# Seven dense groups of 384 and 512 tokens, two low halves on another engine, and a shorter check of limits

## The chip, the cores and the metric

The kernel runs on one core of a Trainium2 chip. The metric is the device time of one execution in microseconds (us); lower is better. TensorE is called PE in the profile, with its weight loads listed apart as PEld; DVE is VectorE, ACT is ScalarE, POOL is GpSimd and SP is SyncE, which here issues most of the transfers.

## The reference

Three layers run one after the other on 3072 tokens of width 384 (4 batches of 768 positions, 8 heads of 48).

```
state = alpha[t] * state + k[t] (x) v[t];  y[t] = q[t] . state      # gated linear attention, per head
noisy = x @ w_gate + log1p(exp(x @ w_noise)) * noise                # 8 experts, the best 2 of each token
out[token] += weight * (relu(x @ w1[e]) @ w2[e])                    # w1: 384 x 1024, w2: 1024 x 384
g = max(0.01 * h, h), h = x @ w_in;  result = g @ w_out             # dense layer, 384 -> 2048 -> 384
```

## The kernel before, in words

**Stages.** Attention runs first, in 24 units of 128 positions. Each unit ends in logits; after every four units a routing chain on DVE (lines 229 to 304 and 1216 to 1258) ranks the experts and gives each choice a slot, and POOL scatters the token rows to the slots by indirect DMA (line 1267). Then the eight experts run, each with two groups of tokens of 320 to 512 rows, then the dense layer with eight groups of 384 tokens. The dense layer fetches its rows by indirect DMA from the experts' outputs (`gather2`, line 830).

**Steps of experts and dense layer.** A group is worked in steps of 128 hidden units. In a step `gemm1` (line 751) makes 9 matmuls whose moving width is the number of tokens of the group (three slices of the 384 inputs, each as high x high, high x low, low x high part). `hidden` then splits the result into a high and a low half: for an expert ACT writes the high half (line 769) and DVE the low one (line 779); in the dense layer ACT copies (line 761), and DVE does the leaky rectifier (764), the high half (771) and the low half (782). `gemm2` (line 799, or 795 for a half block) makes three matmuls of width 384 for each block of 128 tokens. It runs two steps behind `gemm1` (`LAG = 2`); `gemm1` writes to one of two banks (`ph`), and a bank is free when the split of two steps before is done. Four banks (`py`) hold the sums of a group's blocks.

**Weights.** Expert weights come in pairs of 256 hidden units, four pairs for an expert. SP fetches a pair's two halves (`w1s`, `w2s`, two buffers each), ACT makes the high part (`split_hi`, line 504) and DVE or POOL the low part (`split_lo`, line 508). For expert 0 all eight low parts are on POOL, for expert 1 on DVE, for the others wherever the planner finds room.

**Order.** A planner (class `Planner`) places every step in order of time, from durations written into the program, dependences, rings of buffers and due times; each engine's instructions are then issued in that order, and an engine waits at the head of its own queue. Steps of phase 1 may be placed while the attention runs.

**Check of limits.** After the first groups a few sums of counts (`flag_sums`, line 625 ff., on PE into the bank `pA`) are compared with the limits for which the fast path is made (`raise_flag`, lines 632 to 652): 18 small operations on DVE in one planner step. If a limit is broken, a general program runs behind.

```
on = "g" if e == 0 else "v" if e < EARLY else "vg"
add("v", 3.0, raise_flag, use=[(v1, R["pA"])], phase=2, due=tm[0] + 60)
groups += [("b", 0, g) for g in range(N // GROUP2)]
```

Of the kernel before, what the change touches and what calls it, by code (L numbers as in the profile page):

```python
# [28 lines left out]
EARLY = 2  # L29
# [7 lines left out]
SURE, CLEARED = 656, 4  # L37
GROUP2 = 384
F64B = 2
# [334 lines left out]
def tile_kernel(  # L374
# [74 lines left out]
    ones_b = consts.tile([128, 128], BF)  # L449
    zeros = consts.tile([128, Dm], FT)  # L450
    acc = consts.tile([128, NCH + 1, E], BF)
# [7 lines left out]
    msk = {}  # L459

    def route_consts():
        nc.gpsimd.iota(desc, pattern=[[1, E]], base=1, channel_multiplier=0, allow_small_or_imprecise_dtypes=True)
        nc.gpsimd.memset(ones_f, float(E))
        for i in range(2):
            nc.gpsimd.tensor_copy(turn_w[:, :, i * D:(i + 1) * D],
                                  identf[:, None, 64 * i:64 * i + D].to_broadcast([128, HP, D]))
        nc.gpsimd.affine_select(out=tri, in_=ones_f, pattern=[[1, 128]], compare_op=OP.is_gt, fill=0.0,
                                base=0, channel_multiplier=-1)
        nc.gpsimd.memset(ones_b, float(E))
        nc.gpsimd.memset(zeros, 0.0)  # L470
# [108 lines left out]
    def clear():  # L579
        ins = nc.sync.dma_start(x_s[1 + E * SURE:1 + E * CAP, :].rearrange("(m p) d -> p m d", p=128),  # L580
                                zeros[:, None, :].to_broadcast([128, E * (CAP - SURE) // 128, Dm]))
        apart(ins, [other for other, tile_no in scattered if tile_no < CLEARED] + [t for t, _ in taken])
        cleared.append(ins)

    def blocks(key):
        return GB[key[1]][key[2]] if key[0] == "a" else blocks_of(GROUP2)

    GMAX = max(max(max(sizes) for sizes in SIZES), GROUP2)
    XT, XP, bank_of = {}, {}, {}
# [42 lines left out]
    def raise_flag():  # L632
        pf = flags["pf"]
        cm = rt.tile([128, 1], FT, name="cmx")
        nc.vector.tensor_reduce(cm, pf[:, 0:E], axis=AX.X, op=OP.max)
        nc.vector.tensor_scalar(cm, cm, float(E * CAP + E), None, op0=OP.is_le)
        vs = rt.tile([128, 1], FT, name="vs")
        nc.vector.tensor_scalar(vs, pf[:, E:E + 1], 0.0, None, op0=OP.is_le)
        nc.vector.tensor_mul(vs, vs, cm)
        nc.vector.tensor_reduce(cm, pf[:, 0:E], axis=AX.X, op=OP.add)  # L640
        nc.vector.tensor_scalar(cm, cm, float(E * 2 * N + E * (E + 1) // 2), None, op0=OP.is_equal)
        nc.vector.tensor_mul(vs, vs, cm)
        nc.vector.tensor_reduce(cm, pf[:, 0:E], axis=AX.X, op=OP.min)
        nc.vector.tensor_scalar(cm, cm, float(E * SURE), None, op0=OP.is_gt)
        nc.vector.tensor_mul(vs, vs, cm)
        nc.vector.tensor_reduce(cm, pf[:, E + 1 + EARLY:], axis=AX.X, op=OP.max)
        nc.vector.tensor_scalar(cm, cm, float(E * SURE + E), None, op0=OP.is_le)
        nc.vector.tensor_mul(vs, vs, cm)
        for e in range(EARLY):
            nc.vector.tensor_scalar(cm, pf[:, E + 1 + e:E + 2 + e], float(E * SIZES[e][0]), None, op0=OP.is_ge)  # L650
            nc.vector.tensor_mul(vs, vs, cm)
        nc.vector.tensor_scalar(flag, vs, -1.0, 1.0, op0=OP.mult, op1=OP.add)


    groups = [("a", e, g) for g in range(2) for e in range(EARLY)]
    groups += [("a", e, g) for e in range(EARLY, E) for g in range(2)]
    groups += [("b", 0, g) for g in range(N // GROUP2)]
    LAG = 2

    def build_experts(t0, R, scat, cleared_at, ready_at, totals, acc_done, begun):  # L660
# [29 lines left out]
        def expert_weights(i, after):  # L690
# [4 lines left out]
            for m, nm in enumerate(("w1s", "w2s")):  # L695
# [57 lines left out]
        def hidden(si, what):  # L753
# [65 lines left out]
        def rows_stored(gi, j):  # L819
            key = groups[gi]  # L820
            o, n = blocks(key)[j]
            r0 = key[2] * GROUP2 + o
            dst = rows_of(y_d, key[1], key[2], j) if key[0] == "a" else out[r0:r0 + n, :]
            nc.sync.dma_start(dst, YG[gi, j][:n, :])

        def gather2(g, j, kk):
            c = g * (GROUP2 // 128) + j
            rows = 1 + (E * G0 if (c + 1) * 128 <= G0 else E * CAP)
# [4 lines left out]
        def combine(g, j, kk):  # L833
            c = g * (GROUP2 // 128) + j
            ya = YG["b", g, j, 0]
            if kk == 0:
                nc.scalar.activation(ya, ya, AF.Copy, scale=wts[:, c, 0:1])
            else:
                nc.vector.scalar_tensor_tensor(ya, YG["b", g, j, 1], wts[:, c, 1:2], ya, op0=OP.mult, op1=OP.add)
                xg_t["b", 0, g, j] = ya  # L840

        out_rows = {0: [], 1: []}
        xdone, S1, S2 = {}, {}, {}
        t = t0

        def group_in(gi):
# [50 lines left out]
        for si, (gi, f, nf) in enumerate(steps):  # L897
# [666 lines left out]
```

## Time and profile before

| | |
|---|---|
| median of 3 runs | 1033.15 us (1027.29 to 1034.31) |
| the profiled execution | 1029.27 us |
| its span, first to last instruction | 1027.6 us |
| what lies around the span | 1.67 us |
| mean granted TensorE clock | 0.997 |
| busy: PE, DVE, ACT, POOL | 98%, 55%, 37%, 27% |

Busy is the share of the span in which an engine had work. Matmuls are pipelined, so the time of a run of matmuls is read from the distance between their starts, not from their durations.

### The profile page before, as it was taken

Reading aid. Unit: us, or ns where it says so; the run is one execution under the profiler, and the core shown is the slowest. Engines: PE = TensorE matmul, PEld = TensorE weight load, DVE = VectorE, ACT = ScalarE, POOL = GpSimd, SP = SyncE. Lnnn points to the kernel's source line nnn. Section 1 sums busy time; section 2 is a strip of 40 time slices with the busy share of each in tenths; the row PEclk is TensorE's granted clock in tenths of the full one; section 3 lists DMA queues with packets and bytes.
Section 4 is the critical chain, followed back from the end, with each engine's and each line's share of the span. In section 5 each row is a group of like instructions: output and inputs, shape, how many; then the busy total and the mean of one; then the engine's idle time right before and its main releaser. Section 6 shows DMA issues by size and latency. Waiting matters only on the chain.

```text
span 1027.6 us, 17907 instructions
## 1 busy us (share of the span) xinstructions
PE 1005.4 (98%) x6714; PEld 968.6 (94%) x6714; DVE 567.5 (55%) x1270; ACT 384.3 (37%) x815; POOL 277.6 (27%) x310
## 2 busy tenths in 40 slices
PE   8999889999999999999999999999999999999997
PEld 7888779999899999999999999999999999999997
DVE  8999946224745545454543456645454545454543
ACT  5667535223534545353533342313131313121211
POOL 4377776001122324242322244302020202000000
PEclk9999999999999999999999999999999999999999
DMA  9979737325533646454667564302020202010000
GB/s 256 248 251 292 253 136 241 117 89 177 188 113 133 211 141 206 143 182 155 190 215 260 180 210 136 95 1 70 1 70 1 70 1 70 1 40 1 24 1 27
DMA packets 79507, 133.37 MB, mean 130 GB/s; under 512 B 8498, under 2 KB 57140, under 8 KB 79412
## 3 DMA queue, kind: packets, MB, share of 16 engines
q1 hardware_dynamic: 73268, 113.26, 34.9%
q0 software_dynamic: 6144, 18.88, 5.5%
q8 instruction: 55, 0.90, 0.4%
q14 instruction: 40, 0.33, 0.1%
HBM read 92.98 MB, written 39.13 MB: 129 GB/s over the span
## 4 chain that ended last, share of the span: by engine, by line
PE 85%; DVE 7%; DMA 3%; POOL 2%; issue 2%; ACT 1%; SPq 0%; POOLq 0%; DVEq 0%; ACTq 0%
PE ph L751 40%; PE py L799 38%; PE py L795 2%; DVE pT L1016 2%; DVE pF L1009 2%; PE pA L600 1%; DMA at<-in_al_l_dram 1%; PE pB L600 1%; POOL x_s L1267 1%; DVE kt L1030 1%; DVE qp L1036 1%; DMA kq<-in_kq_l_dram 1%; DMA x_s<-xg,si 1%; POOL w1lA L508 1%; PE pA L1161 1%
## 5 line engine op out<-in xcount | busy, mean ns | idle before, releaser
L799 PE MATMUL py<-w2hA,hh 128*128 128x384 f32 x768 | 220.0, 340 | 0.0
L799 PE MATMUL py<-w2hB,hh 128*128 128x384 f32 x768 | 218.7, 338 | 0.0
L779 DVE SCALAR_TENSOR_TENSOR hh<-ph,hh 128x64 fp32r<-128x64 f32 (+2 forms) x192 | 79.4, 442 | 182.7 <-ACT hh L769 182.6
L761 ACT ACTIVATE hc<-ph 128x384 f32<-128x384 f32 x128 | 62.9, 491 | 283.2 <-PE ph L751 283.2
L764 DVE SCALAR_TENSOR_TENSOR hc<-hc 128x384 f32<-128x384 f32 x128 | 72.4, 565 | 168.7 <-ACT hc L761 168.4
L769 ACT ACTIVATE hh<-ph 128x384 fp32r<-128x384 f32 (+3 forms) x128 | 66.3, 518 | 233.6 <-PE ph L751 207.5
L799 PEld LDWEIGHTS py<-w2hA,hh 128*128 128x128 f32 x768 | 141.5, 189 | 0.9
L799 PEld LDWEIGHTS py<-w2hB,hh 128*128 128x128 f32 x768 | 140.9, 188 | 0.7
L751 PE MATMUL ph<-xh,w1hA 128*128 128x384 f32 (+3 forms) x384 | 134.7, 351 | 4.6 <-DVE hh L779 2.8
L751 PE MATMUL ph<-xh,w1lA 128*128 128x384 f32 (+3 forms) x384 | 132.9, 346 | 0.3 <-POOL w1lA L508 0.3
L751 PE MATMUL ph<-xh,w1hB 128*128 128x384 f32 (+1 forms) x384 | 132.7, 346 | 0.0
L751 PE MATMUL ph<-xl,w1hB 128*128 128x384 f32 (+1 forms) x384 | 132.5, 345 | 0.1
L751 PE MATMUL ph<-xl,w1hA 128*128 128x384 f32 (+3 forms) x384 | 132.4, 345 | 0.0
L751 PE MATMUL ph<-xh,w1lB 128*128 128x384 f32 (+1 forms) x384 | 132.3, 344 | 0.0
L799 PE MATMUL py<-w2lA,hh 128*128 128x384 f32 x384 | 130.0, 339 | 0.3 <-POOL w2lA L508 0.3
L799 PE MATMUL py<-w2lB,hh 128*128 128x384 f32 x384 | 128.7, 335 | 0.0
L830 POOL DMA_INDIRECT xg<-y_d,gidx x48 | 49.5, 1031 | 248.0 <-PE pA L600 117.7
L751 PEld LDWEIGHTS ph<-xh,w1hA 128*128 128x128 f32 x384 | 72.4, 189 | 7.0 <-DVE hh L779 2.1
L751 PEld LDWEIGHTS ph<-xh,w1lA 128*128 128x128 f32 x384 | 72.4, 189 | 3.0 <-POOL w1lA L508 0.6
L782 DVE TENSOR_TENSOR hh<-hc,hh 128x384 fp32r<-128x384 f32 x128 | 72.5, 566 | 4.4
L751 PEld LDWEIGHTS ph<-xl,w1hA 128*128 128x128 f32 x384 | 72.4, 189 | 1.5
L751 PEld LDWEIGHTS ph<-xh,w1lB 128*128 128x128 f32 x384 | 72.1, 188 | 1.7
(181 smaller groups left out, 1572.4 us busy)
## 6 DMA issues: line engine op xcount, KB each, us to landing
w1s<-in_moe_w_dram SPq DMA_DIRECT2D x32, 384.0 KB
w2s<-in_moe_w_dram SPq DMA_DIRECT2D x32, 384.0 KB
kq<-in_kq_l_dram SPq DMA_DIRECT2D x24, 448.0 KB
xg<-x_s SPq DMA_DIRECT2D x48, 192.0 KB
y_d<-ys SPq DMA_DIRECT2D x48, 192.0 KB
nv<-in_v_l_dram SPq DMA_DIRECT2D x24, 256.0 KB
w1s<-in_moe_w_in_dram SPq DMA_DIRECT2D x24, 256.0 KB
w2s<-in_moe_w_out_dram SPq DMA_DIRECT2D x16, 384.0 KB
```

Of the source, the lines that this page charges most:

```text
L600: pe.last = nc.tensor.transpose(p[:, d, :n], src[:n, d * 128:(d + 1) * 128], identf[:n, :n])
L751: pe.last = nc.tensor.matmul(ps[:, :n], a[:, d, fo:fo + 128], x[:, d, :n], start=i == 0, stop=i == len(seq) - 1)
L761: nc.scalar.activation(hc[:, :n], ps[:, :n], AF.Copy)
L764: nc.vector.scalar_tensor_tensor(hc[:, :n], hc[:, :n], 0.01, hc[:, :n], op0=OP.mult, op1=OP.max)
L769: nc.scalar.activation(hh[:, :n], ps[:, :n], AF.Relu)
L779: nc.vector.scalar_tensor_tensor(dst, ps[:, a:b], 0.0, hh[:, a:b].bitcast(FT), op0=OP.max, op1=OP.subtract)
L782: nc.vector.tensor_sub(hl[:, :n], HT[si, "hc"][:, :n], hh[:, :n].bitcast(FT))
L795: pe.last = nc.tensor.matmul(py, HT[si, "both"][:, o:o + 128], w[:, f % 2, :], start=(f == 0 and i == 0), stop=(f == nf - 1 and i == 1))
L799: pe.last = nc.tensor.matmul(py[:n, :], h[:, o:o + n], w[:, f % 2, :], start=(f == 0 and i == 0), stop=(f == nf - 1 and i == 2))
L830: return nc.gpsimd.indirect_dma_start(out=yg, out_offset=None, in_=y_d[0:rows, :], in_offset=bass.IndirectOffsetOnAxis(ap=gidx[:, c, kk:kk ...
L1009: nc.vector.tensor_tensor_scan(rev(suf_f[:, 0:NW - 1]), rev(d["at"][:, 1:NW]), rev(heads_f[:, 1:NW]), 1.0, OP.mult, OP.add)
L1016: nc.vector.tensor_tensor_scan(wt, d["at"][:, i * half:(i + 1) * half], heads_f[:, i * half:(i + 1) * half], 0.0, OP.mult, OP.add)
```

## The change

Four edits. The dense layer's eight groups of 384 tokens become seven, of 384, 512, 512, 512, 384, 384 and 384 tokens; the planner's durations for the dense splits scale with the width. For the last two pairs of expert 0 the low halves are made on DVE instead of POOL (four operations; the first two pairs stay on POOL). The check of limits becomes two comparisons of all sums with two rows of limits (prepared at the start by POOL), a sum, a comparison, a count and the flag: six operations, each a planner step of its own. The tile of zeros moves to a pool that ends with the attention.

```diff
-GROUP2 = 384
+GROUPS2 = (384, 512, 512, 512, 384, 384, 384)
...
+    roof, base_ = (consts.tile([128, 2 * E + 1 + EARLY], FT, name=nm) for nm in ("roof", "base_"))
...
-        nc.gpsimd.memset(zeros, 0.0)
+        nc.gpsimd.memset(short["zeros"], 0.0)
...
+        nc.gpsimd.memset(roof, BIG)
+        nc.gpsimd.memset(base_, -BIG)
+        nc.gpsimd.memset(roof[:, 0:E], float(E * CAP + E))
...
+        def above():
+            nc.vector.tensor_tensor(bad[:, 0:n], pf, roof, op=OP.is_gt)
+
+        def below():
+            nc.vector.tensor_tensor(bad[:, n:2 * n], pf, base_, op=OP.is_lt)
+
+        def summed():
+            nc.vector.tensor_reduce(total[:, 0:1], pf[:, 0:E], axis=AX.X, op=OP.add)
+
+        def missing():
+            nc.vector.tensor_scalar(bad[:, 2 * n:], total[:, 0:1], float(E * 2 * N + E * (E + 1) // 2), None, op0=OP.not_equal)
+
+        def counted():
+            nc.vector.tensor_reduce(total[:, 1:2], bad, axis=AX.X, op=OP.add)
+
+        def raised():
+            nc.vector.tensor_scalar(flag, total[:, 1:2], 0.0, None, op0=OP.is_gt)
...
-    groups += [("b", 0, g) for g in range(N // GROUP2)]
+    groups += [("b", 0, g) for g in range(len(GROUPS2))]
...
-                on = "g" if e == 0 else "v" if e < EARLY else "vg"
+                on = "g" if e == 0 and PAIRS[i][2] < 2 else "v" if e < EARLY else "vg"
...
-                hc = HT[si, "hc"] = mw.tile([128, GROUP2], FT, name="hc", bufs=2)
+                hc = HT[si, "hc"] = mw.tile([128, max(GROUPS2)], FT, name="hc", bufs=2)
...
-                hc = add("a", 0.5, lambda si=si: hidden(si, "hc"), use=[(g1, R["ph"])], takes=[R["hc"]], phase=2)
-                lk = add("v", 0.6, lambda si=si: hidden(si, "leak"), use=[(hc, R["hc"])], phase=2)
+                hc = add("a", 0.5 * k, lambda si=si: hidden(si, "hc"), use=[(g1, R["ph"])], takes=[R["hc"]], phase=2)
+                lk = add("v", 0.6 * k, lambda si=si: hidden(si, "leak"), use=[(hc, R["hc"])], phase=2)
...
-                add("v", 3.0, raise_flag, use=[(v1, R["pA"])], phase=2, due=tm[0] + 60)
+                fo = add("v", 0.0, lambda: parts.extend(raise_flag()), [v1], phase=2, due=tm[0] + 60)
+                for k in range(6):
+                    fo = add("v", 0.17, lambda k=k: parts[k](), [fo], use=[(v1, R["pA"])] if k < 3 else [], phase=2,
+                             due=tm[0] + 60 + k)
...
+        zeros = short["zeros"] = ac.tile([128, Dm], FT, name="zeros")
```

## Rows read from the trace of the kernel before

**Rows 1.** The page: busy time by engine, and the chain that ended last.

```profile
PE 1005.4 (98%) x6714; PEld 968.6 (94%) x6714; DVE 567.5 (55%) x1270; ACT 384.3 (37%) x815; POOL 277.6 (27%) x310
PE 85%; DVE 7%; DMA 3%; POOL 2%; issue 2%; ACT 1%; SPq 0%; POOLq 0%; DVEq 0%; ACTq 0%
```

**Rows 2.** Windows: stretch, length, busy us (instructions) by engine, clock, DMA, GB/s.

```profile
140.00:150.00 10.00, 7.30 (x37) 6.75 (x35) 8.53 (x20) 4.72 (x10) 8.18 (x7) 0.83 0.65 213
200.00:225.00 25.00, 25.00 (x132) 22.33 (x131) 5.75 (x10) 5.57 (x11) 0.00 (x0) 1.00 0.35 114
```

**Rows 3.** Timeline of DVE, 264 to 272 us: start, length, operation [idle before].

```profile
264.64 0.17 DVE L635 TENSOR_REDUCE cmx<-pA 128x1 f32<-128x8 f32 x1 [0.66 <-PE pA L630]
...
265.68 1.87 DVE L642 TENSOR_TENSOR vs<-vs,cmx 128x1 f32<-128x1 f32 x1
...
269.95 0.16 DVE L648 TENSOR_TENSOR vs<-vs,cmx 128x1 f32<-128x1 f32 x1
...
270.99 1.01 DVE L779 SCALAR_TENSOR_TENSOR hh<-ph,hh 128x384 fp32r<-128x384 f32 x2
```

**Rows 4.** Timeline of PE, 269 to 272 us.

```profile
269.45 0.34 PE L799 MATMUL py<-w2hB,hh 128*128 128x384 f32 x1
271.59 0.44 PE L751 MATMUL ph<-xh,w1hA 128*128 128x384 f32 x1 [1.80 <-DVE hh L779]
```

**Rows 5.** Timeline of PE, 144 to 162 us: the first matmul behind each wait.

```profile
144.66 0.38 PE L751 MATMUL ph<-xh,w1hA 128*128 128x320 f32 x1 [1.84 <-ACT hh L769]
...
150.10 0.39 PE L751 MATMUL ph<-xh,w1hA 128*128 128x320 f32 x1 [0.95 <-DVE hh L779]
...
159.58 0.41 PE L751 MATMUL ph<-xh,w1lA 128*128 128x320 f32 x1 [0.31 <-POOL w1lA L508]
...
161.36 0.44 PE L799 MATMUL py<-w2lA,hh 128*128 128x384 f32 x1 [0.32 <-POOL w2lA L508]
```

**Rows 6.** Timeline of POOL, 142 to 164 us: low halves of expert 0.

```profile
142.15 1.84 POOL L508 TENSOR_TENSOR w2lA<-w2s,w2hA 128x768 fp32r<-128x768 f32 x1
...
146.43 1.85 POOL L508 TENSOR_TENSOR w1lA<-w1s,w1hA 128x768 fp32r<-128x768 f32 x1
...
157.68 1.85 POOL L508 TENSOR_TENSOR w1lA<-w1s,w1hA 128x768 fp32r<-128x768 f32 x1
159.47 3.62 POOL L508 TENSOR_TENSOR w2lA<-w2s,w2hA 128x768 fp32r<-128x768 f32 x2
```

**Rows 7.** Timeline of DVE, 141 to 157 us.

```profile
141.47 2.58 DVE L240 SCALAR_TENSOR_TENSOR g_um<-g_u,g_ex 128x32 f32<-128x32 f32 x1
...
145.77 2.58 DVE L302 SCALAR_TENSOR_TENSOR g_rest<-g_oh,g_z 128x32 f32<-128x32 f32 x1
...
149.41 1.01 DVE L779 SCALAR_TENSOR_TENSOR hh<-ph,hh 128x64 fp32r<-128x64 f32 x4
152.16 0.56 DVE L779 SCALAR_TENSOR_TENSOR hh<-ph,hh 128x64 fp32r<-128x64 f32 x2 [1.75 <-ACT hh L769]
...
155.87 0.95 DVE L508 TENSOR_TENSOR w1lB<-w1s,w1hB 128x768 fp32r<-128x768 f32 x1
```

**Rows 8.** Timeline of ACT, 143 to 159 us: two high halves of expert 0.

```profile
143.12 0.84 ACT L504 ACTIVATE w1hA<-w1s 128x768 fp32r<-128x768 f32 x1 [0.94 <-DMA w1s<-in_moe_w_dram]
...
157.65 0.84 ACT L504 ACTIVATE w2hA<-w2s 128x768 fp32r<-128x768 f32 x1
```

**Rows 9.** Chain of waits: start, length, nine matmuls of one gemm1.

```profile
199.65 2.08 PE ph L751 x9
...
671.86 1.56 PE ph L751 x9
...
704.36 1.59 PE ph L751 x9
```

**Rows 10.** Groups by line: busy us, mean ns, idle before and its releaser.

```profile
L764 DVE SCALAR_TENSOR_TENSOR hc<-hc 128x384 f32<-128x384 f32 x128 | 72.4, 565 | 168.7 <-ACT hc L761 168.4
```

**Rows 11.** Timeline of POOL at the start.

```profile
9.60 1.24 POOL L1080 TENSOR_SCALAR_AFFINE_SELECT am<-ar 128x512 f32<-128x512 f32 x2 [5.43 <-ACT ar L1075]
```

More of the change, by code (lines that the diff above doesn't have):

```diff
@@ L449, in tile_kernel @@
     ones_b = consts.tile([128, 128], BF)
-    zeros = consts.tile([128, Dm], FT)
     acc = consts.tile([128, NCH + 1, E], BF)
@@ L456, in tile_kernel @@
     flag = consts.tile([128, 1], I32)
+    roof, base_ = (consts.tile([128, 2 * E + 1 + EARLY], FT, name=nm) for nm in ("roof", "base_"))
     m_all, pk_all = (consts.tile([128, 2, NCH], FT, name=nm) for nm in ("m_all", "pk_all"))
-    msk = {}
+    msk, short = {}, {}
     def route_consts():
@@ L469, in route_consts @@
         nc.gpsimd.memset(ones_b, float(E))
-        nc.gpsimd.memset(zeros, 0.0)
+        nc.gpsimd.memset(short["zeros"], 0.0)
         nc.gpsimd.memset(acc, 0.0)
         nc.gpsimd.tensor_scalar(acc[0:1, 0, :], desc[0:1, :], 1.0 / E, None, op0=OP.mult)
+        nc.gpsimd.memset(roof, BIG)
+        nc.gpsimd.memset(base_, -BIG)
+        nc.gpsimd.memset(roof[:, 0:E], float(E * CAP + E))
+        nc.gpsimd.memset(base_[:, 0:E], float(E * SURE + 1))
+        nc.gpsimd.memset(roof[:, E:E + 1], 0.0)
+        for e in range(EARLY):
+            nc.gpsimd.memset(base_[:, E + 1 + e:E + 2 + e], float(E * SIZES[e][0]))
+        nc.gpsimd.memset(roof[:, E + 1 + EARLY:], float(E * SURE + E))
         for n in sorted({NG * len(g) for g in RGROUPS}):
@@ L580, in clear @@
         ins = nc.sync.dma_start(x_s[1 + E * SURE:1 + E * CAP, :].rearrange("(m p) d -> p m d", p=128),
-                                zeros[:, None, :].to_broadcast([128, E * (CAP - SURE) // 128, Dm]))
+                                short["zeros"][:, None, :].to_broadcast([128, E * (CAP - SURE) // 128, Dm]))
         apart(ins, [other for other, tile_no in scattered if tile_no < CLEARED] + [t for t, _ in taken])
@@ L585, in blocks @@
     def blocks(key):
-        return GB[key[1]][key[2]] if key[0] == "a" else blocks_of(GROUP2)
-    GMAX = max(max(max(sizes) for sizes in SIZES), GROUP2)
+        return GB[key[1]][key[2]] if key[0] == "a" else blocks_of(GROUPS2[key[2]])
+    GMAX = max(max(max(sizes) for sizes in SIZES), max(GROUPS2))
     XT, XP, bank_of = {}, {}, {}
@@ L632, in raise_flag @@
     def raise_flag():
[L633 to L651, printed above, removed]
@@ L652, in raise_flag @@
-        nc.vector.tensor_scalar(flag, vs, -1.0, 1.0, op0=OP.mult, op1=OP.add)
+        pf, n = flags["pf"], 2 * E + 1 + EARLY
+        bad = rt.tile([128, 2 * n + 1], FT, name="bad", bufs=1)
+        total = rt.tile([128, 2], FT, name="vs")
+        def above():
[4 more added lines that the diff above has]
+            nc.vector.tensor_reduce(total[:, 0:1], pf[:, 0:E], axis=AX.X, op=OP.add)
@@ L655, in tile_kernel @@
+        def missing():
[4 more added lines that the diff above has]
+            nc.vector.tensor_scalar(flag, total[:, 1:2], 0.0, None, op0=OP.is_gt)
+        return [above, below, summed, missing, counted, raised]
     groups = [("a", e, g) for g in range(2) for e in range(EARLY)]
     groups += [("a", e, g) for e in range(EARLY, E) for g in range(2)]
-    groups += [("b", 0, g) for g in range(N // GROUP2)]
+    groups += [("b", 0, g) for g in range(len(GROUPS2))]
@@ L658, in tile_kernel @@
+    assert sum(GROUPS2) == N
+    START2 = [sum(GROUPS2[:g]) // 128 for g in range(len(GROUPS2))]
     LAG = 2
@@ L821, in rows_stored @@
             o, n = blocks(key)[j]
-            r0 = key[2] * GROUP2 + o
+            r0 = START2[key[2]] * 128 + o
             dst = rows_of(y_d, key[1], key[2], j) if key[0] == "a" else out[r0:r0 + n, :]
@@ L826, in gather2 @@
         def gather2(g, j, kk):
-            c = g * (GROUP2 // 128) + j
+            c = START2[g] + j
             rows = 1 + (E * G0 if (c + 1) * 128 <= G0 else E * CAP)
@@ L833, in combine @@
         def combine(g, j, kk):
-            c = g * (GROUP2 // 128) + j
+            c = START2[g] + j
             ya = YG["b", g, j, 0]
@@ L840, in combine @@
                 xg_t["b", 0, g, j] = ya
+        parts = []
         out_rows = {0: [], 1: []}
@@ L851, in group_in @@
                 for j in range(len(blocks(key))):
-                    c = key[2] * (GROUP2 // 128) + j
+                    c = START2[key[2]] + j
                     deps = ready_at[c] + out_rows[0] + ([] if (c + 1) * 128 <= G0 else out_rows[1])
@@ L919, in build_experts @@
             else:
-                hc = add("a", 0.5, lambda si=si: hidden(si, "hc"), use=[(g1, R["ph"])], takes=[R["hc"]], phase=2)
-                lk = add("v", 0.6, lambda si=si: hidden(si, "leak"), use=[(hc, R["hc"])], phase=2)
-                hh = add("v", 0.47, lambda si=si: hidden(si, "hh"), [lk], use=[(hc, R["hc"])], takes=[R["hh"]], phase=2)
-                hl = add("v", 0.63, lambda si=si: hidden(si, "hl"), use=[(hc, R["hc"]), (hh, R["hh"])], phase=2)
+                hc = add("a", 0.5 * k, lambda si=si: hidden(si, "hc"), use=[(g1, R["ph"])], takes=[R["hc"]], phase=2)
+                lk = add("v", 0.6 * k, lambda si=si: hidden(si, "leak"), use=[(hc, R["hc"])], phase=2)
+                hh = add("v", 0.47 * k, lambda si=si: hidden(si, "hh"), [lk], use=[(hc, R["hc"])], takes=[R["hh"]], phase=2)
+                hl = add("v", 0.63 * k, lambda si=si: hidden(si, "hl"), use=[(hc, R["hc"]), (hh, R["hh"])], phase=2)
             S1[si].update(hh=hh, hl=hl)
```

## The prediction

> **What bounds the kernel now.** I read the page first: PE is busy for 98% of the span and makes 85% of the chain that ended last, while DVE has work for 55% and POOL for 27% [rows 1]. An edit of the other engines can therefore only pay where PE waits for them, and PE itself can only gain where it needs less time for the same columns. So I looked next, by windows, for stretches in which PE is not full. Behind the attention there are two. One is the hand-over to expert 0: from 140 to 150 us PE is busy for 7.30 of 10 us, and its granted clock means 0.83 [rows 2]. The other is at 270 us, and the timelines show both from near: each matmul that follows a wait carries the idle time and what ended it. At 270 us PE waits 1.80 us for a low half on DVE [rows 4]. In the hand-over it waits 1.84 us (released by ACT), 0.95 us (DVE) and 0.31 and 0.32 us (two low halves of weights on POOL) [rows 5]. That is 5.2 us of idle time in all, and it is nearly everything that the other engines still owe PE.
>
> **The check of limits.** On DVE it runs from 264.64 us until the next low half begins at 270.99, so 6.35 us [rows 3]. The planner gives it 3.0 us. The difference is mostly one pattern: an operation that needs 0.16 us alone (L648) took 1.87 us as L642, while POOL made low halves of weights. PE's last matmul starts at 269.45, the next at 271.59 [rows 4]; with some 0.17 us for the last one, 2.0 us are lost, of which 1.80 are booked as a wait. After the change there are six operations at 0.16 to 0.17 us each, about 1.0 us, and other work of DVE can go between them. If one of them still meets POOL, add 1.7 us (1.87 less 0.16): 2.7 us. Before, a hold of 6.35 us cost 1.80, so the slack is some 4.5 us, and neither 1.0 nor 2.7 reaches it. The gain is **1.8 us**, bounds 0 (the six land beside other late work) and 2.0. I take 1.8, since what is left is well inside the slack.
>
> The Trainium skill bears on the 1.87 us ("SBUF — State Buffer", section "SBUF: two separate sides"): VectorE and GpSimd share a pair of ports, and a VectorE operation with two SBUF inputs is held for the whole of a GpSimd operation that reads SBUF. The trace agrees: L642 has two SBUF inputs and lasts as long as POOL's low half, 1.85 us. By the page the new check would not be held at all, since its two comparisons read one operand from PSUM; my sum would be the same.
>
> **The four low halves.** Each takes POOL 1.8 us [rows 6], and on DVE one of the same shape takes 0.95 us [rows 7]: DVE gets 3.8 us more, POOL 7.2 to 7.4 less. Two of PE's waits end with these very operations, those of 0.31 and 0.32 us [rows 5]. DVE is idle for 1.75 us just before 152.16 [rows 7], so there is room to make them earlier: **0.6 us** gained. The wait of 0.95 us ends with the low half at 149.41, which stands behind L302: 2.58 us from 145.77, next to POOL's low half at 146.43 to 148.28 [rows 6, 7]. That low half moves to DVE. If nothing takes its place on POOL, L302 is free of it, but DVE has 0.95 us more to do, twice if the next one comes along as well. POOL's next low half (`w2l` of pair 1) stays there and can move up into the same place. I take half, **0.5 us**, bounds 0.95 gained and 1.9 lost (two low halves ahead of the split, none saved). The first wait, 1.84 us, ends behind L240, 2.58 us beside POOL's low half at 142.15 [rows 6, 7]; that one stays on POOL, so I take nothing. If the new order removed it, the idle time and the clock that falls with it would go: a mean of 0.83 over 10 us between the levels of 2.4 and 1.2 GHz is 3.4 us at the lower one, or 1.7 us of lost work [rows 2]. Bounds: 3.5 us gained, or 1.6 lost (a second fall of clock as costly as this one, if the other wait grows to its size). SP's fetches of the next pairs wait for these halves and move up; no wait of PE in the rows ends with a fetch.
>
> **The dense layer.** Blocks of 128 tokens, transposes, gathers, evictions and `gemm2` are as many as before. Only `gemm1` changes: 16 steps x 3 groups = 48 steps of 9 matmuls of width 512 replace 64 of width 384. Nine of width 512 take 2.08 us; nine of width 384 take 1.56 us in some stretches of the dense layer and 1.59 in others [rows 9]. Four thirds of 1.56 is 2.08, of 1.59 is 2.12. So a step gains 0 to 0.04 us, and 48 steps gain 0 to 1.9 us. I take the middle, **1.0 us**, since both levels occur. Below zero: if the wide steps meet a slower level too, as 1.59 stands to 1.56 (2%), 48 x 2.08 x 2% = 2.0 us are lost.
>
> Per matmul 512 columns take 231 ns and 384 take 173 to 177, so nearly all the time goes by columns and little is saved by issuing fewer. The Trainium skill ("TensorE: Matmul & The Clock Gate", section "Wait — 56ns, not 53.3ns?") gives columns at 2.4 GHz plus a fixed 2.5 ns for each matmul; an estimate from that page is 144 x 2.5 ns = 0.4 us, which would replace my 1.0. The rows agree that the fixed part is small, though their 231 ns lies above its 216.
>
> DVE's work per step grows by a third, and so does the step. Of 128 dense steps DVE waits 168.7 us for the first split [rows 10], 1.3 us a step, so cover remains; gone, the price would be what is missing of those 1.3 us, 48 times. Groups of four blocks fill all four banks `py`. Around 200 to 225 us such groups follow one another, and PE is busy for 25.00 of 25.00 us [rows 2]; the evictions hide behind two steps. A late one would cost its own wait, three times. The second dense group needs eight gathers instead of six while the first runs, 16 steps of about 3.15 us.
>
> **At nothing.** Eight more small fills on POOL at the start: POOL then idles 5.43 us before its first mask [rows 11], far above what fills of 19 columns need; uncovered, they would delay the first unit by their length. The tile of zeros in another pool: its last reader runs during the attention, before the space is used again; otherwise every first expert tile would wait for that transfer.
>
> **The sum.** 1.8 + 0.6 + 0.5 + 1.0 = 3.9 us less. The profiled execution took 1029.27 us, 1.67 more than its span of 1027.6; it becomes 1025.4. The median of the runs is 1033.15, 3.9 us above the profiled one, and would become 1029.2. The four times known (1027.29, 1029.27, 1033.15, 1034.31) spread over more than the sum. Their middle is 1031.2; less 3.9 that is 1027.3, and I state **1028**, between that and the median's.
>
> **Rivals.**
> (a) *The hand-over clears altogether*, chance 0.15. With four low halves fewer POOL is early, and DVE is never held. For it: three of the waits are tied to low halves on POOL [rows 5 to 7]. Against: the first two pairs stay there. Gain 1.8 + 0.6 + 0.95 + 3.5 + 1.9 = 8.8 us, from 1031.2 to 1022.4.
> (b) *The ports take it back*, chance 0.2. A moved low half reads two SBUF inputs, like L240 and L302, which were held for 2.4 us each [rows 7]; it meets the one that stays on POOL, and the wait of 0.95 grows by 1.9 us. Sum: 1.8 + 0.6 - 1.9 + 1.0 = 1.5 us gained, 1029.7. This is the page's port rule as it would speak against the change, and the stretched L240 and L302 bear it out.
> (c) *Slower: a new wait at the head of DVE's queue*, chance 0.15. DVE works in order. ACT makes a high half of `w2` for expert 0 only at 157.65 us [rows 8]. Should the planner expect it sooner, and put its low half directly behind the split at 152.16 [rows 7], the next splits of the hidden units would stand behind it from 152.7 to 159.4 (157.65 + 0.84 + 0.95). DVE held for 3.6 us (145.77 to 149.41) cost PE 0.95, so the slack here is 2.7 us and beyond it every us counts. A hold of 6.7 us costs 4.0, and the clock's fall 1.7 more: 5.7 lost against 3.4 gained (1.8 + 0.6 + 1.0), net 2.3 slower, 1033.5. It decides from a hold of about 6 us on. Against it: the planner knows the fetch and ACT's time, if roughly.
> The forecast has the remaining 0.5.
>
> **Range and chances.** From the lower runs' level with most of (a) to the upper runs' level with (c) cut short: 1020 to 1034 us. About 1% is what a measurement can tell here. Over 1% faster means below 1022.8: half of (a), and a little of the forecast on a fast chip, 0.09. Over 1% slower means above 1043.5, for which no case has the price: 0.02. Within 1%: 0.89.
>
> **What would show it.** In the changed profile: no wait of PE for a low half near 270 us, and six short operations where 6.35 us were; no wait of PE released by POOL between 155 and 165 us; low halves of 0.95 us on DVE in the hand-over, and whether L302 still takes 2.58; nine matmuls of width 512 at 2.08 us in the dense layer. A wait of PE for DVE of over 2 us between 140 and 165 us, or any at the edge of a 512-token group, would make the prediction wrong.

## The result, and the profile after

The changed kernel takes 1020.86 us (median of 6 runs, 1020.34 to 1022.16), the kernel before 1034.54 us in 6 runs beside it (1027.29 to 1037.35). The ratio is 0.9875, with a 95% interval of 0.9843 to 0.9907. The profiled execution took 1020.34 us with a span of 1018.6, 8.9 us less than that of before. The forecast was 1028, from 1020 to 1034: the direction was right and the time lies at the low end of the range, but the gain is over twice the 3.9 us of my sum. Note the spread: the times of before lie over 10 us, those of after over 2.

The page's busy times and chain answer to [rows 1]:

```profile
PE 1001.2 (98%) x6570; PEld 948.7 (93%) x6570; DVE 559.1 (55%) x1219; ACT 379.9 (37%) x795; POOL 270.3 (27%) x313
PE 89%; DVE 5%; DMA 2%; issue 1%; ACT 1%; POOL 1%; SPq 0%; POOLq 0%; ACTq 0%; DVEq 0%
```

PE's share of the chain grew from 85 to 89%: less of the end is set by others. The windows (columns as in [rows 2]) show where:

```profile
140.00:150.00 10.00, 8.16 (x42) 7.92 (x42) 7.51 (x23) 4.40 (x8) 7.06 (x6) 0.83 0.67 225
150.00:160.00 10.00, 10.00 (x69) 9.80 (x68) 8.43 (x23) 4.63 (x10) 6.65 (x7) 1.00 0.80 275
250.00:300.00 50.00, 50.00 (x288) 48.68 (x287) 25.15 (x55) 22.79 (x47) 9.33 (x9) 1.00 0.48 161
```

From 150 us on PE is full (859.9 of the 860 us to 1010). Of the waits of [rows 4, 5] one is left, the first, and the granted clock still means 0.83 around it. In the timeline of PE, 138 to 164 us:

```profile
143.16 0.38 PE L764 MATMUL ph<-xh,w1hA 128*128 128x320 f32 x1 [1.84 <-ACT hh L782]
```

The timeline of DVE answers to [rows 7], and its rows from 264 us to [rows 3] (L516 is now the low half of a weight, L792 that of the hidden units, L1245 the scan of the routing chain):

```profile
139.96 2.58 DVE L240 SCALAR_TENSOR_TENSOR g_um<-g_u,g_ex 128x32 f32<-128x32 f32 x1
...
144.27 0.19 DVE L302 SCALAR_TENSOR_TENSOR g_rest<-g_oh,g_z 128x32 f32<-128x32 f32 x1
...
145.15 0.22 DVE L1245 TENSOR_TENSOR_SCAN run<-msk,ot 128x32 bf16<-128x32 bf16 x1
145.98 0.95 DVE L516 TENSOR_TENSOR w1lA<-w1s,w1hA 128x768 fp32r<-128x768 f32 x1
...
264.03 0.18 DVE L646 TENSOR_TENSOR bad<-pA,roof 128x19 f32<-128x19 f32 x1
264.28 0.56 DVE L792 SCALAR_TENSOR_TENSOR hh<-ph,hh 128x384 fp32r<-128x384 f32 x1
...
267.54 0.15 DVE L661 TENSOR_SCALAR flag<-vs 128x1 int32<-128x1 f32 x1
```

L240 is held as before, L302 is not: 0.19 us for 2.58. The six operations of the check take 0.15 to 0.18 us each, and a split of the hidden units goes between them. POOL's rows for 130 to 150 us say why L302 is free. Its low half of pair 1 comes at 148.35, after the routing chain, since it stands in POOL's queue behind a scatter that waited 2.44 us for a matmul. The last row is POOL's low half beside the check:

```profile
140.66 1.83 POOL L516 TENSOR_TENSOR w2lA<-w2s,w2hA 128x768 fp32r<-128x768 f32 x1
...
147.36 0.97 POOL L1285 DMA_INDIRECT x_s<-xg,si  x1 [2.44 <-PE py L812]
148.35 1.86 POOL L516 TENSOR_TENSOR w2lA<-w2s,w2hA 128x768 fp32r<-128x768 f32 x1
...
263.81 1.91 POOL L516 TENSOR_TENSOR w1lB<-w1s,w1hB 128x768 fp32r<-128x768 f32 x1 [28.75 <-ACT w1hB L512]
```

The first comparison (264.03, 0.18 us), with one input from PSUM (`pA`), ran while POOL was busy with that low half, and was not held.

To lay executions side by side I cut each at the starts of ACT's splits of the experts' steps (ACT's timeline) and of the dense layer (the first split of each step). Before and after, in us:

| stretch | before | after | less |
|---|---|---|---|
| start to step 0 | 141.73 | 140.25 | 1.48 |
| step 0 to 8 (hand-over) | 26.17 | 23.81 | 2.36 |
| step 8 to 34 | 96.47 | 96.18 | 0.29 |
| step 34 to 37 (check) | 12.90 | 10.88 | 2.02 |
| step 37 to 120 | 301.25 | 300.19 | 1.06 |
| step 120 to the last dense step | 438.10 | 436.05 | 2.05 |
| rest of the execution | 12.65 | 12.98 | -0.33 |

Their sum is 8.93. Two lines have a place in my sum (hand-over 1.1, check 1.8). The dense layer gained twice its 1.0, and 1.3 us came off the experts' steps, for which I had no term.

### The profile page after: what moved, and what is told of

Its sections match the earlier page's. It is cut to its first block, busy times and chain, and to the rows that moved or that the text cites. A ratio compares the mean times of both kernels' runs of the same rounds, so it can differ in the third digit from the quotient of the medians.

```text
span 1018.6 us, 17522 instructions
## 1 busy us (share of the span) xinstructions
PE 1001.2 (98%) x6570; PEld 948.7 (93%) x6570; DVE 559.1 (55%) x1219; ACT 379.9 (37%) x795; POOL 270.3 (27%) x313
## 4 chain that ended last, share of the span: by engine, by line
PE 89%; DVE 5%; DMA 2%; issue 1%; ACT 1%; POOL 1%; SPq 0%; POOLq 0%; ACTq 0%; DVEq 0%
PE ph L764 41%; PE py L812 40%; PE py L808 2%; DVE pF L1027 1%; DVE pT L1034 1%; PE pA L608 1%; PE pB L608 1%; PE pA L1179 1%; PE pY L1149 1%; PE pY L1156 1%; DMA at<-in_al_l_dram 1%; PE pS L1089 1%; DMA x_s<-xg,si 1%; DVE qp L1054 1%; DVE kt L1048 1%
## 5 line engine op out<-in xcount | busy, mean ns | idle before, releaser
L792 DVE SCALAR_TENSOR_TENSOR hh<-ph,hh 128x64 fp32r<-128x64 f32 (+2 forms) x192 | 79.6, 442 | 182.7 <-ACT hh L782 181.9
L774 ACT ACTIVATE hc<-ph 128x384 f32<-128x384 f32 (+1 forms) x112 | 60.0, 536 | 292.4 <-PE ph L764 292.4
L777 DVE SCALAR_TENSOR_TENSOR hc<-hc 128x384 f32<-128x384 f32 (+1 forms) x112 | 69.9, 624 | 173.1 <-ACT hc L774 173.0
L764 PE MATMUL ph<-xh,w1hA 128*128 128x384 f32 (+3 forms) x360 | 129.3, 359 | 1.8 <-ACT hh L782 1.8
L764 PE MATMUL ph<-xl,w1hB 128*128 128x384 f32 (+2 forms) x360 | 128.0, 356 | 0.1
L764 PE MATMUL ph<-xh,w1hB 128*128 128x384 f32 (+2 forms) x360 | 127.9, 355 | 0.0
L764 PE MATMUL ph<-xh,w1lB 128*128 128x384 f32 (+2 forms) x360 | 127.9, 355 | 0.0
L812 PEld LDWEIGHTS py<-w2lA,hh 128*128 128x128 f32 x384 | 72.5, 189 | 1.5
L812 PEld LDWEIGHTS py<-w2lB,hh 128*128 128x128 f32 x384 | 72.2, 188 | 1.4
L764 PEld LDWEIGHTS ph<-xh,w1lA 128*128 128x128 f32 x360 | 67.6, 188 | 5.4
L795 DVE TENSOR_TENSOR hh<-hc,hh 128x384 fp32r<-128x384 f32 (+1 forms) x112 | 70.0, 625 | 3.7
```

The source lines that it names most:

```text
L764: pe.last = nc.tensor.matmul(ps[:, :n], a[:, d, fo:fo + 128], x[:, d, :n], start=i == 0, stop=i == len(seq) - 1)
L777: nc.vector.scalar_tensor_tensor(hc[:, :n], hc[:, :n], 0.01, hc[:, :n], op0=OP.mult, op1=OP.max)
L792: nc.vector.scalar_tensor_tensor(dst, ps[:, a:b], 0.0, hh[:, a:b].bitcast(FT), op0=OP.max, op1=OP.subtract)
L795: nc.vector.tensor_sub(hl[:, :n], HT[si, "hc"][:, :n], hh[:, :n].bitcast(FT))
L812: pe.last = nc.tensor.matmul(py[:n, :], h[:, o:o + n], w[:, f % 2, :], start=(f == 0 and i == 0), stop=(f == nf - 1 and i == 2))
```

## The experiments

**E1, the kernel before once more.** No edit; it tells what an execution does by itself.

> The kernel before, unchanged, against itself. The medians differ by 13.7 us, the two profiled executions by 8.9 us. Theory A (a cost that the kernel before pays in most executions and not in the profiled one, some 5 us): most times lie at 1033 to 1037 us, few at 1027 to 1029, and a profile of a slow execution shows the 5 us in waits of PE or in its clock, near 140 to 160 us or at 270 us. Theory B (a slow chip or chance): the times scatter evenly, and no stretch of the profile stands out.

Measured: 1029.89 us (12 runs, 1027.24 to 1035.82), ratio 0.9982 (0.9961 to 1.0004). Its first split came at 140.26 us, 1.47 before the 141.73 of the table: the first line of the table needs no edit. But the hand-over took 30.65 us instead of 26.17. Its PE, DVE and POOL timelines, 143 to 151 us:

```profile
143.20 0.38 PE L751 MATMUL ph<-xh,w1hA 128*128 128x320 f32 x1 [1.84 <-ACT hh L769]
...
150.76 0.60 PE L751 MATMUL ph<-xh,w1hA 128*128 128x320 f32 x1 [4.61 <-DVE hh L779]
```

```profile
144.31 2.57 DVE L302 SCALAR_TENSOR_TENSOR g_rest<-g_oh,g_z 128x32 f32<-128x32 f32 x1
...
147.58 2.34 DVE L1227 TENSOR_TENSOR_SCAN run<-msk,ot 128x32 bf16<-128x32 bf16 x1
149.95 0.19 DVE L1230 TENSOR_TENSOR acc<-run,acc 128x32 bf16<-128x32 bf16 x1
150.06 1.01 DVE L779 SCALAR_TENSOR_TENSOR hh<-ph,hh 128x64 fp32r<-128x64 f32 x4
```

```profile
144.98 1.84 POOL L508 TENSOR_TENSOR w1lA<-w1s,w1hA 128x768 fp32r<-128x768 f32 x1
146.99 0.99 POOL L1267 DMA_INDIRECT x_s<-xg,si  x1 [0.17 <-issue]
148.01 1.82 POOL L508 TENSOR_TENSOR w2lA<-w2s,w2hA 128x768 fp32r<-128x768 f32 x1
```

Here DVE is held twice, by two low halves in a row, and PE's second wait is 4.61 us instead of 0.95. What was different in the execution of [rows 5] stands in POOL's rows of the kernel before, from 149 us:

```profile
149.43 0.99 POOL L1267 DMA_INDIRECT x_s<-xg,si  x1 [1.15 <-PE py L795]
150.44 1.87 POOL L508 TENSOR_TENSOR w2lA<-w2s,w2hA 128x768 fp32r<-128x768 f32 x1
```

POOL's scatter waited for a matmul there, and that matmul was late, since the clock fell right behind the first wait: matmuls of width 320 start 0.27 us apart from 145.07 on, in E1 0.15. So the next low half came at 150.44, behind the routing chain; in E1 the scatter waited for nothing, and the low half met the scan. The kernel before has two kinds of hand-over, a cheap and a dear one, and the profile that I predicted from shows the cheap one. The two kinds alone do not make the spread: the twelve times lie all over their 9 us. The windows of E1 show the clock fall after the long wait instead:

```profile
140.00:150.00 10.00, 4.30 (x27) 3.75 (x25) 9.59 (x15) 3.97 (x8) 9.13 (x7) 0.96 0.67 226
150.00:160.00 10.00, 9.24 (x45) 9.14 (x46) 3.90 (x17) 2.16 (x5) 1.82 (x2) 0.70 0.29 100
```

**E2, the new check alone.** The kernel before with `raise_flag`, its planner steps and its two rows of limits from the change.

> Only the check of limits in six operations. By the profiles it is worth 2.0 us (theory A0: nothing more, ratio 0.998). Theory A1: the wait of PE at 270 us also costs clock in most executions of the kernel before, so the median falls by 3.5 to 6 us. A rival, that the check is hidden anyway: 0.

Measured: 1025.73 us (1023.73 to 1028.69), ratio 0.9932 (0.9911 to 0.9953). Steps 34 to 37 take 10.88 us, 2.0 less than before and 1.4 less than in E1 (12.31), and no wait is left there. The hand-over is of the dear kind (30.60). Yet steps 37 to 120 take 300.18 (before 301.25) and the dense steps, first to last, 402.59 (before 403.85), where nothing was edited; of PE's instructions only the sums for the check stand elsewhere. It begins ahead of the check: steps 8 to 34 take 96.19 us for 96.47. The median lies 6.9 us below that of the kernel before in the same set (1032.64), more than the 4.3 us by which this profiled execution is shorter than E1's; E5 shows what can make a difference, the fall of the clock that theory A1 supposed.

**E3, the four low halves alone.**

```
-on = "g" if e == 0 else "v" if e < EARLY else "vg"
+on = "g" if e == 0 and PAIRS[i][2] < 2 else "v" if e < EARLY else "vg"
```

> Only the four low halves of expert 0 on DVE. By the profiles 2.4 us are gained between the first and the ninth step of expert 0, so the median falls by 2.4 us (theory A0). Theory A2: in most executions of the kernel before the hand-over costs more clock than in the profiled one, and the median falls by 4 to 7 us. Rival (DVE's queue): 0 or slower.

Measured: 1026.48 us (1023.39 to 1029.35), ratio 0.9935 (0.9912 to 0.9958). The hand-over takes 23.37 us, 2.8 less than the cheap kind and 7.3 less than the dear one (23.81 in the changed kernel, where the clock fell). PE has the first wait of 1.84 and no other in the hand-over; L302 takes 0.19 and the scan 0.23. Steps 37 to 120 stay at 301.25 and the dense steps at 403.85. The granted clock stays at 1.00 from 140 to 160 us.

**E4, the dense groups alone** (with the move of the tile of zeros).

```
-GROUP2 = 384
+GROUPS2 = (384, 512, 512, 512, 384, 384, 384)
```

> Only the seven dense groups (with the tile of zeros in the attention's pool, as in the change). By the profiles 1.9 us are gained between the first and the last step of the dense layer (theory A0). Theory A3: most of what the other two do not give comes from here, 5 us or more, by other places of tiles in memory or by the waits at the groups' edges. Rival: 0, since time goes by columns.

Measured: 1031.8 us (12 runs, 1026.37 to 1033.47), ratio 0.9982 (0.9962 to 1.0002). First to last dense step 403.23 us for 403.85: **0.6 us**, not the expected 1.9. The hand-over is of the cheap kind (26.18), with the clock at 0.83 from 140 to 150 us. Nine wide matmuls take 2.08 us in 24 rows of the chain and 2.10 or 2.11 in 24.

**E5, the second set of tiles moved by 32 bytes.** The new rows of limits move every tile that comes after them in SBUF. The first guess for the unexplained gain was the offset from a multiple of 64 bytes.

```
+spare = rt.tile([128, 8], FT, name="spare", bufs=1)
+nc.vector.memset(spare, 0.0)
```

> The kernel before with one unused tile of 32 bytes per partition in the routing pool (and one small fill): the second set of weights, one of the two sets of input rows and the hidden halves then start 32 bytes past a multiple of 64, as all others do and as in the kernel with the six-operation check. No other order of work. Theory P (places of tiles): the steps from expert 2 on gain 2.5 us as in the kernel with the check alone (1.0 in the experts, 1.5 in the dense layer). Theory Q (the new check's order made that gain): no change from expert 2 on. Both: hand-over and the wait at 270 us as before.

Measured: 1031.22 us (12 runs, 1028.42 to 1037.08), ratio 0.9992 (0.9969 to 1.0015). Steps 37 to 120 took 301.66 us, 0.4 more, and the dense steps 403.35, 0.5 less: no gain on the whole. The hand-over was of the dear kind (30.65). Steps 34 to 37 took 14.47 us, where the kernel before, with a wait of the same length, needs 12.90: here the granted clock fell behind the check's wait of 1.79 us. The windows of E5, and then of the kernel before:

```profile
270.00:280.00 10.00, 8.21 (x40) 7.70 (x40) 7.78 (x18) 4.30 (x8) 2.70 (x2) 0.83 0.61 196
```

```profile
270.00:280.00 10.00, 8.41 (x51) 8.07 (x52) 8.44 (x22) 4.55 (x12) 0.57 (x1) 1.00 0.55 174
```

So the old check costs 2.0 us with this wait where the clock holds, 1.4 with the wait of 1.21 us in E1, and 3.6 in this execution.

**E6, the changed kernel with all tiles at multiples of 64 bytes** (an unused tile of 32 bytes in `consts`).

> The changed kernel with one unused tile of 32 bytes per partition among the constants, so that all weights, rows and hidden halves start on a multiple of 64 bytes. Theory P1 (equal offset is what counts): no change. Theory P2 (a multiple of 64 is better than 32 past it): the 128 expert steps and 112 dense steps gain, up to 6 us if every matmul of width 384 goes from 176 to 173 ns. Theory Q: no change.

Measured: 1021.0 us (1019.26 to 1022.05), ratio 0.9893 (0.9867 to 0.992). Steps 37 to 120 take 300.20, the dense steps 402.04, as in the changed kernel. With E5, the offset from a multiple of 64 bytes is out as the cause.

**E7, all eight low halves on DVE.**

```
-on = "g" if e == 0 and PAIRS[i][2] < 2 else "v" if e < EARLY else "vg"
+on = "v" if e < EARLY else "vg"
```

> The changed kernel with all eight low halves of expert 0 on DVE, so that POOL makes none in the hand-over. Theory port: the operation L240 beside POOL's low half falls from 2.58 to 0.2 us, the wait of 1.84 us and the fall of the clock behind it go, 3.5 us gained. Rival: DVE, with 3.8 us more to do, is late for the first steps itself, and the first wait stays or grows: 0 to 3 us slower.

Measured: 1025.26 us (1024.36 to 1028.1), ratio 0.9943 (0.9922 to 0.9964), 4 us slower than the changed kernel. Its DVE rows from 143 us, then the one wait of PE behind the attention:

```profile
143.82 0.19 DVE L240 SCALAR_TENSOR_TENSOR g_um<-g_u,g_ex 128x32 f32<-128x32 f32 x1
...
147.69 0.19 DVE L1248 TENSOR_TENSOR acc<-run,acc 128x32 bf16<-128x32 bf16 x1
147.80 1.01 DVE L792 SCALAR_TENSOR_TENSOR hh<-ph,hh 128x64 fp32r<-128x64 f32 x4
```

```profile
148.50 0.61 PE L764 MATMUL ph<-xh,w1hA 128*128 128x320 f32 x1 [3.33 <-DVE hh L792]
```

L240 is free now. But the first split came at 145.22 us, 5.0 later than in the changed kernel and 2.1 later than in the latest of the other runs (140.20 to 143.11). While DVE made the extra low halves, POOL's work for the attention was stretched: a mask took 1.39 us at 132.52 and 0.65 at 135.60. And the planner put the split of the hidden units behind the whole routing chain, so the first wait grew to 3.33.

**E8, the changed kernel with eight dense groups of 384.**

```
-GROUPS2 = (384, 512, 512, 512, 384, 384, 384)
+GROUPS2 = (384,) * 8
```

> The changed kernel with eight dense groups of 384 tokens again. Theory A0: the wide groups alone were worth 0.6 us in the profile of the kernel that had them alone, so 0.6 us slower from the first to the last dense step (ratio to the changed kernel 1.0006, not to be seen in the times). By the prediction's middle 1.0; by 1.9 if the steps of width 384 stand at their slower level now.

Measured: 1021.19 us (1019.47 to 1022.14), ratio 0.9893 (0.9867 to 0.992). First to last dense step 402.59 us, 402.00 with the wide groups: 0.6 us again. In this execution the clock stayed at 1.00 behind the first wait, and steps 0 to 34 took 118.79 us instead of 119.99: by these two executions the fall of the clock costs 1.2 us there.

**E9, the kernel before with its tiles where E2 has them.** Unused tiles of 192 and 96 bytes put every tile of the experts and the dense layer at E2's addresses.

```
+spare_c = consts.tile([128, 48], FT, name="spare_c")
+nc.gpsimd.memset(spare_c, 0.0)
...
+spare = rt.tile([128, 24], FT, name="spare", bufs=1)
+nc.vector.memset(spare, 0.0)
```

> The kernel before with two unused tiles (192 and 96 bytes a partition), so that every weight, row and split tile of the experts and the dense layer lies at the same address as in the kernel that has the new check of limits alone. Theory Place: the 2.5 us by which kernels with the new check are quicker apart from their wait (1.0 between steps 40 and 120 of the experts, 1.4 in the dense layer) come from where the tiles lie; then this kernel shows them too: steps 40 to 120 in 289.6 us instead of 290.6, ratio about 0.9975. Rival: they come from the program itself (its instructions, its 12 operations fewer on DVE); then steps 40 to 120 stay at 290.6 and the ratio is 1.000. Either way the check still costs its 2 us between steps 34 and 37 (12.3 to 12.9, not 10.9).

Measured: 1031.05 us (12 runs, 1028.19 to 1034.09), ratio 1.0001 (0.9978 to 1.0023). The ratio shows nothing: its interval begins just above the expected 0.9975. Its profiled execution has the dear hand-over, with this wait of PE:

```profile
152.67 0.61 PE L755 MATMUL ph<-xh,w1hA 128*128 128x320 f32 x1 [4.63 <-DVE hh L783]
```

The times do not bear the gain out, the stretches do. Steps 40 to 120 take 289.59 us (before and E1 290.61), the dense steps 402.59 (403.85, 403.86); from step 8 to the last dense step it needs 845.58 us where E1 needs 848.15, 2.6 less. PE's matmuls come in the same order in E9 and in the kernel before. The five profiled executions without new tiles (before, E1, E3, E4, E10) take 290.61 or 290.62 us for steps 40 to 120, the eight with the tiles of the check or with E9's 289.59 to 289.62. Theory Place holds in the profiled executions: where the tiles lie is worth **2.6 us**, spread over 850 us of matmuls. The chain's rows show the price as lengths of 1.56 to 1.59 us: of 250 pieces of nine matmuls of width 384 between 615 and 1020 us, 103 took 1.59 us before, 43 here, and 43 in E2, another program with its tiles at the same places.

**E10, one low half moved.** Only w1 of expert 0's third pair goes to DVE.

```
-on = "g" if e == 0 else "v" if e < EARLY else "vg"
+on = "v" if e == 0 and m == 0 and PAIRS[i][2] == 2 else "g" if e == 0 else "v" if e < EARLY else "vg"
```

> The kernel before with one low half moved, w1 of expert 0's third pair, from POOL to DVE; the other seven stay on POOL. Theory Hold: this is the POOL operation beside which L302 (2.58 us) and in the other kind of hand-over the scan L1227 (2.34 us) are held; without it the routing chain ends before POOL's next low half, the wait of 0.95 us or of 4.61 us goes in both kinds, and steps 0 to 8 take about 24 us instead of 26.2 or 30.7, nearly as much as with all four halves moved (23.4); the waits of 0.31 and 0.32 us for POOL may stay. Time 2 to 3 us under the kernel before, ratio about 0.994 to 0.997. Rival Load: what counts is POOL's total work (each low half 1.8 us), so a quarter of it gives a quarter: steps 0 to 8 stay over 25.5 us and the ratio is 0.998 or more.

Measured: 1028.26 us, ratio 0.9973 (0.9952 to 0.9994). Eleven of twelve runs lie between 1027.37 and 1029.16, the twelfth at 1032.88. The rows of DVE, PE and POOL, 145 to 159 us:

```profile
145.06 0.19 DVE L302 SCALAR_TENSOR_TENSOR g_rest<-g_oh,g_z 128x32 f32<-128x32 f32 x1
...
145.95 0.23 DVE L1227 TENSOR_TENSOR_SCAN run<-msk,ot 128x32 bf16<-128x32 bf16 x1
...
152.57 5.77 DVE L1257 CAST si<-pk_all 128x8 uint32<-128x8 f32 x1 [0.18 <-DVE pk_all L1253]
158.26 1.01 DVE L779 SCALAR_TENSOR_TENSOR hh<-ph,hh 128x64 fp32r<-128x64 f32 x4
```

```profile
158.94 0.38 PE L751 MATMUL ph<-xh,w1hA 128*128 128x320 f32 x1 [3.05 <-DVE hh L779]
```

```profile
151.92 0.97 POOL L1267 DMA_INDIRECT x_s<-xg,si  x1 [0.30 <-PE pA L1242]
152.91 1.86 POOL L508 TENSOR_TENSOR w1lA<-w1s,w1hA 128x768 fp32r<-128x768 f32 x1
154.71 3.59 POOL L508 TENSOR_TENSOR w2lA<-w2s,w2hA 128x768 fp32r<-128x768 f32 x2
```

Theory Hold is right on the mechanism: one operation taken off POOL frees L302 and the scan, the waits of 0.95 and of 4.61 are both gone, and so is most of the spread in these twelve runs. It missed the size: steps 0 to 8 take 25.93 us, not 24, since a cast of 8 columns, 0.17 to 0.21 us elsewhere, is now held 5.77 us until POOL's three low halves are done, and PE waits 3.05 us behind it. This is what rival (c) described, a hold at the head of DVE's queue, in another place.

The Trainium skill ("SBUF — State Buffer", section "SBUF: two separate sides") says that the shared ports go, for a whole instruction, to whichever of VectorE and GpSimd starts first, and counts among VectorE's claimants those with two SBUF inputs and those in a faster mode that uses both ports. That L302 and the scan, with two inputs in SBUF, are held until POOL's low half is done agrees (E1: 144.31 + 2.57 us and 144.98 + 1.84). That the first to start is served does not show here: in E1's rows both start 0.4 to 0.7 us before the low half that holds them, though spans on POOL are rough. The cast has one input; that it is in such a mode is not shown by any row here.

**E11, a fifth low half on DVE**: w2 of the first pair, the one beside L240.

```
-on = "g" if e == 0 and PAIRS[i][2] < 2 else "v" if e < EARLY else "vg"
+on = "g" if e == 0 and PAIRS[i][2] < 2 and (m == 0 or PAIRS[i][2] == 1) else "v" if e < EARLY else "vg"
```

> The changed kernel with a fifth low half on DVE: w2 of expert 0's first pair, beside which L240 is still held for 2.58 us in it. Theory Hold: L240 then takes 0.2 us, the split before PE's first expert step comes up to 2 us sooner, the wait of 1.84 us and the fall of the clock behind it go: 1.8 to 3.5 us quicker than the changed kernel, about 1018, ratio 0.985. Rival Crowd (what the kernel with all eight on DVE showed): the extra low half on DVE stretches the end of the attention, PE's first expert step starts later, and a new wait for DVE replaces the old one: as slow as the changed kernel or up to 4 us slower, 1021 to 1025.

Measured: 1021.9 us (1019.46 to 1023.61), ratio 0.9915 (0.9883 to 0.9946); the changed kernel's is 0.9875 (0.9843 to 0.9907), so no gain can be seen. DVE and PE, 140 to 144 us:

```profile
140.04 0.19 DVE L240 SCALAR_TENSOR_TENSOR g_um<-g_u,g_ex 128x32 f32<-128x32 f32 x1
...
142.83 0.26 DVE L1248 TENSOR_TENSOR acc<-run,acc 128x32 bf16<-128x32 bf16 x1
143.10 1.02 DVE L792 SCALAR_TENSOR_TENSOR hh<-ph,hh 128x64 fp32r<-128x64 f32 x4
```

```profile
143.81 0.60 PE L764 MATMUL ph<-xh,w1hA 128*128 128x320 f32 x1 [2.54 <-ACT w2hA L512]
```

L240 is free, as Hold said, and the wait grew from 1.84 to 2.54 us, as Crowd said: the split now stands behind the last operation of the routing chain, which ends at 143.09. The wait is booked on ACT, but the first half of the split on DVE ends just as late (143.10 + 0.5 us). Freeing the held operation was not enough; the order on DVE took the gain.

**E12, the changed kernel with its first set of tiles at the old offset from a multiple of 256 bytes** (an unused tile of 64 bytes in `consts`).

> The changed kernel with an unused tile of 64 bytes a partition, so that the first set of weights and the rows of the first buffer lie at 160 bytes past a multiple of 256, as in the kernel before, instead of 96 (every other tile of the experts moves by the same 64 bytes). Theory Place, with this offset as the cause: the 2.5 us come back, steps 40 to 120 take 290.6 us instead of 289.6, the dense layer from its first to its last step takes about 403 us instead of 402.0, and the time is about 1023.4 us, ratio 0.992. Rival: it is not this offset but another tile's place, or the distance between tiles; then steps 40 to 120 stay at 289.6 and the time at 1021.

Measured: 1021.19 us (1020.62 to 1021.53), ratio 0.9912 (0.9884 to 0.994). Steps 40 to 120 take 289.61, the dense steps 402.06: the rival holds, this offset is not the cause. **Still open** is which tile's place, or which distance between tiles, it is. E9 moved all tiles by 192 or 288 bytes and added one fill on POOL and one on DVE at once; E5, with a fill on DVE, gained nothing, but POOL's fill was not tried by itself. E6 and E12 add a fill on POOL to the changed kernel, and change nothing.

None of these beats the changed kernel by more than the runs can tell.

## Why the prediction was right or wrong

**The check: right.** 1.8 us forecast, 2.0 measured (E2, and steps 34 to 37 of the table); 1.4 against E1. The slack that I worked out from [rows 3, 4] held. The first comparison met POOL's low half and was not held, and the planner left POOL one low half there (1.91 us) where it had two (3.84 us from 265.67 on). What I left out: the clock can fall behind this wait too, which I priced for the hand-over alone; in E5 that makes 3.6 us.

**The waits on POOL: right, but priced low.** The two waits of 0.31 and 0.32 us are gone in E3 and in the changed kernel, while E1, with the old placement of the halves, has them both. At 270 us I had counted 2.0 us lost for 1.80 booked; in the hand-over I took the booked idle time alone. These rows of the kernel before are PE's last ones ahead of the second, third and fourth wait of [rows 5]:

```profile
148.81 0.34 PE L795 MATMUL py<-w2lA,hh 128*128 128x384 f32 x1
...
158.97 0.31 PE L751 MATMUL ph<-xl,w1hA 128*128 128x320 f32 x1
...
160.71 0.34 PE L799 MATMUL py<-w2hA,hh 128*128 128x384 f32 x1
```

From each of them to the next start it is 1.29, 0.61 and 0.65 us, where 0.17, 0.15 and 0.17 are usual: 2.06 us lost. The start after that comes 0.07 to 0.12 us late each time, which makes 2.35, as much as the 2.36 of the table.

**Half of the wait of 0.95: the step that failed.** I took 0.5 us, on the ground that POOL's next low half could move up beside L302. It did not: behind the scatter that waits for PE it comes at 148.35, after the chain, and the whole wait went; with E1's kind of hand-over 4.61 us went. Together the four halves are worth 2.8 us against the cheap kind and 7.3 against the dear one (E3: 26.17 and 30.65 less 23.37), not 1.1. The dear kind could not be read from the one execution that I had, but its sign could: the four times spread over 7 us, and I averaged over that spread where I should have asked which wait can differ between executions. It is also a part of why the medians differ by 13.7 us and the profiled executions by 8.9: with this hold gone most of the spread went in E10. It is not the whole. E3, without the hold, still spreads over 6 us, E2, with the new check alone, over 5, and the changed kernel, with both edits, over 1.8; the fall of the clock at the old check (E5) can be a second cause. How often either comes, no run shows.

**The first wait: right.** I took nothing, and 1.84 us and the clock's fall stayed [rows 2, 5]. E11 and E7 show why it would not have been had for the moving: with L240 free it became 2.54 and 3.33.

**The dense layer: a size.** The wide groups gave 0.6 us (E4, E8), in my bounds of 0 to 1.9 and under the 1.0 that I took; the wide steps have levels too, 2.08 and 2.10 (E4), as I allowed below zero. DVE's cover remained; the row that answers to [rows 10]:

```profile
L777 DVE SCALAR_TENSOR_TENSOR hc<-hc 128x384 f32<-128x384 f32 (+1 forms) x112 | 69.9, 624 | 173.1 <-ACT hc L774 173.0
```

Its idle time is 1.5 us a step, 1.3 before. The Trainium skill's fixed 2.5 ns a matmul ("TensorE: Matmul & The Clock Gate", section "Wait — 56ns, not 53.3ns?") made 0.4, which was nearer.

**The term that was missing.** The paragraph on what costs nothing priced the fills and the move of the tile of zeros, but not that new tiles move all others. By E9's profiled execution that was worth 2.6 us, more than the check. [Rows 9] held the trace of it, 1.56 and 1.59 us for the same nine matmuls, and I read it only as uncertainty of the wide groups.

**The sum again.** By these terms: hand-over 2.4, check 2.0, wide groups 0.6, places 2.6, and 1.5 of an earlier first split, which executions of the same kernel show too (E1). That makes 9.1 of the 8.9 us; the 0.3 of the table's last line, and 0.2 the other way between step 120 and the end of the dense layer, are not explained. The time lies in my range, but partly by luck: the range reached so far down for rival (a), which did not come, and neither the places nor the dear hand-over was in it.

**The rivals.** (a) gave the nearest time, 1022.4, by the wrong way: the hand-over did not clear. (b) did not come: the moved halves were on DVE when POOL had little to do. (c) did not come in the changed kernel, only in E10; its hold of "about 6 us" leaves out the clock's fall that its price has in it, and with the fall 4.4 us would have decided (2.7 + 3.4 - 1.7).

## What to carry to other kernels

Where the times of one kernel spread by more than the sum of an argument, look for a wait that two engines' order of arrival decides, and take a second profile before pricing it. A short operation on DVE with two inputs in SBUF, beside a long one on POOL, should be priced by about the long one's length (1.3 to 2.6 us here beside 1.8 to 1.9); an operation with an input from PSUM was not held, a cast with one input was (E10). But freeing it pays only if the order on its engine lets the urgent work go first. When an edit adds a tile, compare stretches that it does not touch.

## What was not expected of the hardware

- The same nine matmuls of width 384 took 1.56 to 1.59 us at a granted clock of 1.00, and how many took how long changed with the addresses of the tiles (103 of 250 at 1.59 before, 43 in E9). What in the addresses does it is open.
- A cast of 8 columns with one input was held 5.77 us through three back-to-back low halves of POOL, with no gap between them in which it ran (E10).
- A fall of the granted clock behind a short wait made one execution quicker than others: by delaying POOL it spared DVE a hold (26.17 us in [rows 5]'s hand-over, 30.65 in E1's). In the six profiled executions with the old order of the hand-over it goes together each time: 26.17 and 26.18 us where the clock fell behind the first wait (before, E4), 30.60 to 30.99 where it did not (E1, E2, E5, E9).
